# Bucketed attention and a rational feed-forward layer on one core: one weight load moved in the queue, and the last step's four banks finished and stored in turn

## The chip, the cores and the metric

The kernel runs on one core of one Trainium2 chip. The metric is the device time of one execution in microseconds. The core has five engines that this text names as the profile does: PE (TensorE, with its weight loads as PEld), DVE (VectorE), ACT (ScalarE), POOL (GpSimd) and SP (SyncE, which issues most of the DMAs; ACT issues a few).

## The reference, cut to what matters

Attention works on 4 batches of 8 heads, 768 rows, 64 columns. Every row of q and k falls into one of 64 buckets by the signs of six projections; a query sees only the keys of its own bucket. The result, seen as 3072 tokens of 512, goes through a feed-forward layer whose nonlinearity is a quotient of two polynomials.

```
mask   = q_bucket[:, :, :, None] == k_bucket[:, :, None, :]
scores = np.where(mask, scale * np.matmul(q, k.transpose(0, 1, 3, 2)), -1000000000.0)
attn   = np.exp(scores - np.max(scores, axis=-1, keepdims=True))
attn   = attn / (np.sum(attn, axis=-1, keepdims=True) + 1e-09)
x      = np.matmul(attn, v)            # as (3072, 512)
h      = x @ w_in                      # (3072, 2048)
P, Q   = a[0] + a[1]*h + a[2]*h2 + a[3]*h3,  1 + |b[0]| |h| + |b[1]| h2
out    = (P / (Q + 1e-6)) @ w_out      # (3072, 512)
```

The weights w_in and w_out are 64-bit floats; the kernel gets their bits as integers.

## The kernel before, in words

**Two stages.** The first (`attention`) takes the 32 heads as 16 pairs, 0 to 15, each in 12 steps of scores (two halves of the queries times six blocks of 128 keys). The second (`Ffn`) takes the tokens in 6 blocks of 512 (`NBLK`), each in 16 steps `f` of 128 hidden columns (`NFC`).

**How full precision is kept.** An operand is split into a high part in the format that PE takes and the rest, a low part; a product is the sum of high x high, high x low and low x high. So x becomes `xh` and `xl`, the quotient becomes `gh` and `gl`, and w_in and w_out become pairs too.

**A pair.** `maxstep` computes one block of scores of a later pair on PE into a PSUM tile `psm` and takes its row maxima on DVE (`m`). `shift_turn` turns the maxima with PE (`pst`), DVE writes them as `mt`, and `shift_rows` moves them by DMA into an extra row of the operand q (`q<-mt`: the rows of shifts). `scores` computes the blocks `pss` with two matmuls each, and ACT takes their exponential into one of seven buffers `E`. `values` multiplies `E` with `v` into `psv`, in groups of six steps (24 matmuls). POOL, and DVE in the last pairs, add up the `E` (`acc`) for the row sums (`psu`). From step 8 of pair 14 on, two of three score blocks (`wide`, `third`) use the PSUM tiles `psa`, two in number, which `psm` and `pst` use as well; the others use three tiles `s`.

**Operands of the next pair.** `second_low` and `second_high` copy parts of the split operands by DMA (`q<-lo`, `k<-lo`, `q<-q`, `k<-k`), `load_v` loads `v`, `values_store` writes the result of a pair to DRAM (`x_d<-xo`).

**Weights beside the attention.** `weights(i)` is a generator that brings one chunk of 128 x 512 of w_in (even `i`) or w_out (odd `i`): the load into `wr` (`wr<-w_in`, 512 KB), then from 64 to 32 bits with two ACT operations (`ws<-wr`, `wr<-wr`) and three on DVE (`wr<-wr`, `ws<-ws,wr`, and a custom instruction `ws<-wr,ws`), then the split: ACT casts the high part (`wi_hi<-ws`), DVE subtracts for the low one (`wi_lo`). There are two buffers `wr` and two `ws`. Two chunks go with every pair.

**First tokens.** While pairs 14 and 15 run, `Tokens.load` fetches the first block's x: `xl<-x_d` and `xh<-r_d` by DMA, the product `y` on DVE, the cast back to `xh` on ACT, and the subtraction into `xl` on DVE. `y` takes the buffer `lo0` or `lo1`, in which `second_low` finds its source.

**What sets the order.** Every engine carries out its instructions in the order in which the program emits them. In the attention stage this comes from the dictionary `plan` (lines 474 to 589): `at(p, s, f)` puts a piece of work at time 12 p + s, in units of steps, and the program is emitted in order of these times. The tables `MID`, `FIRST` and `LAST` hold the times. The chunk with index 28 = 2 * NFC - 4 is the w_in chunk of pair 14; its load stands at 1.44 steps into pair 14 (time 169.44). Each DMA takes one of eight semaphores in turn, and an issue waits until the DMA that had the semaphore before has landed.

**A step of the feed-forward stage.** `step(i)` emits the first product of step i (12 matmuls, `psh`), the polynomial terms on ACT and DVE, then for step i-1 the quotient (ACT: logarithm and exponential of the denominator, DVE: three operations, ending with `c<-w,c`), for step i-2 `parts` (ACT casts `gh`, POOL subtracts for `gl`, lines 705 to 710), and for step i-4 `gemm2`: 12 matmuls into four banks `pso`, one for each 128 tokens, two with gh and one with gl each, accumulated over the 16 steps. After the 16th step each bank is complete; `store` negates it into SBUF and stores it (`out<-o`).

**The end.** In the last two steps of the last block (`f >= NFC - 2`) all eight matmuls with gh come first and the four with gl last (line 718). ACT empties banks 0 and 2, DVE bank 1; bank 3 is split into two halves of 256 columns (`oh`): ACT empties the first and issues its store from its own queue, DVE the second, stored by SP.

Of the kernel before, what the change touches and what calls it, by code (L numbers as in the profile page):

```python
# [7 lines left out]
F32 = mybir.dt.float32  # L8
# [4 lines left out]
AF = mybir.ActivationFunctionType  # L13
ALU = mybir.AluOpType
# [4 lines left out]
P = 128  # L19
# [9 lines left out]
DM = 512  # L29
DFF = 2048  # L30
NCC = DM // P
NFC = DFF // P
NTK = 512
NBLK = TOK // NTK
# [27 lines left out]
LAST = dict(  # L62
    group=6, values=[0.28, 0.44], values_out=1.39, vout14=3.03,
    tokens=[[-15.0, -11.5, -8.6, -7.4], [-7.43, -5.11, -2.83, -1.09], [1.1, 4.2, 5.45, 6.3]], terms=1.0, ffn=[13.61, 16.09, 16.14],
    sums=16.96, wide=8, share=11, third=0, sums14=14.69, sumst14=22.46,
)
TINY = 2.0 ** -80

# [35 lines left out]
def bucket_attention_then_rational_ffn(ctx, tc, qT, kT, v, proj, w_in, w_out, coef, consts, out):  # L104
# [56 lines left out]
    def operands_to_terms():  # L161
# [3 lines left out]

    tail.tile([P, 32], F32, tag="below", name="below")
    last = attention(tc, nc, raw, ps_b, tail, tokens, early, operands_to_terms, ffn, load, QF, KF, v, w_in, w_out, wo_d, ident, cst,
                     ones, prj, wi_hi, wi_lo, x_d, s_d, r_d, coefficients)
    ffn.rest(ctx, last)
# [3 lines left out]
def attention(ctx, tc, nc, raw, ps_b, tail, tokens, early, operands_to_terms, ffn, load, QF, KF, v, w_in, w_out, wo_d, ident, cst, ones, prj,  # L173
# [305 lines left out]
    def spread(p, steps, gen):  # L479
        for s in steps:  # L480
            at(p, s, lambda g: next(g, None), gen)

    for p in range(NPAIR):
        mid = 0 < p < NPAIR - 1
        n = MID["group"] if mid else (FIRST if p == 0 else LAST)["group"]
# [36 lines left out]
    for i in range(2 * NFC):  # L522
        o = 12 * (i // 2)
        w = list(FIRST["weights"][i]) if i < 2 else list(MID["weights"][i % 2])
        if i == 2 * NFC - 1:
            w = w[:-4] + [w[-5] + x for x in MID["weights_last"]]
        spread(0, [o + x for x in w], weights(i))
# [134 lines left out]
class Ffn:  # L662
# [42 lines left out]
    def parts(self, t, f):  # L705
        p = self.state[t, f]
        gh, gl = self.tile("gh", t, f, 3, F32R), self.tile("gl", t, f, 3, F32R)
        self.nc.scalar.copy(gh, p)
        self.nc.gpsimd.tensor_tensor(out=gl, in0=p, in1=gh.bitcast(F32), op=ALU.subtract)
        self.state[t, f] = gh, gl  # L710

    def gemm2(self, t, f):
        nc = self.nc
        gh, gl = self.state.pop((t, f))
        n, end = NTK // P, (t, f) == (NBLK - 1, NFC - 1)

        order = [(i, k) for i in range(n) for k in range(3)]
        if t == NBLK - 1 and f >= NFC - 2:
            order.sort(key=lambda ik: ik[1] == 2)
        for i, k in order:  # L720
            if f == 0 and k == 0:
                self.sums[t, i] = self.ps_o.tile([P, DM], F32, tag="pso", name=f"pso{t}_{i}")
            g, w = ((gh, 0), (gh, 1), (gl, 0))[k]
            nc.tensor.matmul(self.sums[t, i], g[:, i * P : i * P + P], self.wo[f][:, w, :], start=(f == 0 and k == 0),
                             stop=(f == NFC - 1 and k == 2))
            if f == NFC - 1 and k == 2:
                if end and i == n - 1:
                    self.store(t, i, 0, DM // 2, "scalar", nc.scalar)
                    self.store(t, i, DM // 2, DM, "vector", nc.sync)
                else:  # L730
                    self.store(t, i, 0, DM, "vector" if end and i % 2 else "scalar", nc.sync)

    def store(self, t, i, c0, c1, engine, queue):
        nc = self.nc
        if c1 - c0 < DM:
            o = self.tp.tile([P, DM], F32, tag="h2", name=f"oh{c0}_{t}_{i}", bufs=2)[:, 0 : c1 - c0]
        else:
            tag, bufs = ("sr", 1) if i % 3 == 2 else ("xo", 2)
            o = self.rows.tile([P, DM], F32, tag=tag, name=f"o{t}_{i}", bufs=bufs)[:, 0 : c1 - c0]
        ps = self.sums[t, i][:, c0:c1]  # L740
        if engine == "scalar":
            nc.scalar.activation(o, ps, AF.Identity, scale=-1.0)
        else:
            nc.vector.tensor_scalar(out=o, in0=ps, scalar1=-1.0, scalar2=None, op0=ALU.mult)
        r0 = t * NTK + i * P
        queue.dma_start(self.out[r0 : r0 + P, c0:c1], o)

    def step(self, i):
        seq = [(t, f) for t in range(NBLK) for f in range(NFC)]
# [82 lines left out]
```

## Time and profile before

| what | value |
|---|---|
| time, median of 3 runs | 932.71 us (932.42 to 933.77) |
| the profiled execution's own time | 931.52 us |
| its span on the core | 929.7 us |
| PE busy | 920.8 us (99%) |
| DVE, ACT, POOL busy | 840.8 us (90%), 647.7 us (70%), 436.5 us (47%) |
| DMA queue of SP | 110.47 MB |
| granted clock of TensorE | 1.00 of full speed in all stretches up to 900 us |

Times in the profile count from the span's start. A row of the timeline gives start, duration, engine, the line (line 93 is that of a helper that issues all instructions, so instructions are told apart by their tiles), the operation, out<-in by the program's names, the shapes, how many instructions are merged in the row, and in brackets how long the engine stood idle before it and what ended that. A row of the busy times by stretches gives for one stretch its length, the busy time of PE, PEld, DVE, ACT and POOL with the number of instructions, the granted clock, the mean busy share of the 16 DMA engines, and GB/s. SPq and ACTq are the queues of these engines, and their rows show the issue of a DMA, not its transfer. In the text a time with a point such as 361.11 is a place in the span.

### The profile page before, as it was taken

Reading aid. Unit: us, or ns where it says so; the run is one execution under the profiler, and the core shown is the slowest. Engines: PE = TensorE matmul, PEld = TensorE weight load, DVE = VectorE, ACT = ScalarE, POOL = GpSimd, SP = SyncE. Lnnn points to the kernel's source line nnn. Section 1 sums busy time; section 2 is a strip of 40 time slices with the busy share of each in tenths; the row PEclk is TensorE's granted clock in tenths of the full one; section 3 lists DMA queues with packets and bytes.
Section 4 is the critical chain, followed back from the end, with each engine's and each line's share of the span. In section 5 each row is a group of like instructions: output and inputs, shape, how many; then the busy total and the mean of one; then the engine's idle time right before and its main releaser. Section 6 shows DMA issues by size and latency. Waiting matters only on the chain.

```text
span 929.7 us, 13698 instructions
## 1 busy us (share of the span) xinstructions
PE 920.8 (99%) x4678; PEld 699.3 (75%) x4678; DVE 840.8 (90%) x1029; ACT 647.7 (70%) x1229; POOL 436.5 (47%) x362
## 2 busy tenths in 40 slices
PE   8999999999999999999999999999999999999997
PEld 4666766666767676668888888888888888888886
DVE  6799889788988897887998999999999989998996
ACT  7567767676767676886777667776676677677664
POOL 5587878777878877622222232222223222222222
PEclk9999999999999999999999999999999999999999
DMA  6867877887877777545402100400040003001001
GB/s 197 213 182 225 229 221 230 214 232 220 232 218 220 220 193 228 166 158 189 165 1 86 51 1 1 136 1 0 1 137 1 1 38 98 1 1 46 1 1 46
DMA packets 51242, 111.57 MB, mean 120 GB/s; under 512 B 9346, under 2 KB 20214, under 8 KB 51172
## 3 DMA queue, kind: packets, MB, share of 16 engines
q1 hardware_dynamic: 50740, 110.47, 40.2%
q8 instruction: 37, 0.61, 0.3%
q14 instruction: 33, 0.27, 0.1%
q10 hardware_dynamic: 432, 0.23, 0.1%
HBM read 56.82 MB, written 21.17 MB: 84 GB/s over the span
## 4 chain that ended last, share of the span: by engine, by line
PE 92%; DVE 3%; DMA 3%; SPq 1%; issue 1%; ACT 1%; DVEq 0%; ACTq 0%
PE psh L93 28%; PE pso L93 28%; PE pss L93 13%; PE psv L93 12%; PE psm L93 7%; PE psu L93 2%; DVE m L93 2%; PE psb L93 1%; SPq L93 1%; DMA wr<-w_in 1%; DMA q<-q 1%; DVE ws L93 1%; DVE wr L93 0%; DMA qkf<-kT 0%; DMA xh<-r_d 0%
## 5 line engine op out<-in xcount | busy, mean ns | idle before, releaser
L93 POOL TENSOR_TENSOR gl<-c,gh 128x512 fp32r<-128x512 f32 x96 | 134.6, 1402 | 388.3 <-ACT gh L93 378.9
L93 ACT ACTIVATE E<-pss 128x384 f32<-128x384 f32 x384 | 167.7, 493 | 104.3 <-PE pss L93 93.8
L93 PE MATMUL pso<-wo,gh 128*128 128x512 f32 x768 | 235.5, 389 | 0.0
L93 DVE TENSOR_REDUCE m<-psm 128x1 f32<-128x768 f32 x192 | 179.4, 948 | 30.7 <-PE psm L93 27.6
L93 POOL TENSOR_TENSOR acc<-E,E 128x384 f32<-128x384 f32 x124 | 154.1, 1261 | 84.5 <-ACT E L93 84.4
L93 PE MATMUL pss<-q,k 128*128 128x384 f32 (+2 forms) x768 | 171.2, 346 | 0.4 <-ACT E L93 0.3
L93 PEld LDWEIGHTS pso<-wo,gh 128*128 128x128 f32 x768 | 144.1, 188 | 29.9
L93 PEld LDWEIGHTS pss<-q,k 128*128 128x128 f32 (+2 forms) x768 | 134.5, 189 | 29.2 <-issue 17.0
L93 PE MATMUL psh<-xh,wi_hi 128*128 128x512 f32 x384 | 149.6, 390 | 0.0
L93 PE MATMUL psh<-xl,wi_hi 128*128 128x512 f32 x384 | 149.4, 389 | 0.0
L93 PE MATMUL psh<-xh,wi_lo 128*128 128x512 f32 x384 | 149.4, 389 | 0.0
L93 PE MATMUL pso<-wo,gl 128*128 128x512 f32 x384 | 148.4, 389 | 0.0
L93 ACT ACTIVATE h<-psh 128x512 f32<-128x512 f32 x96 | 57.4, 598 | 127.5 <-PE psh L93 127.4
L93 POOL TENSOR_TENSOR acc<-acc,E 128x384 f32<-128x384 f32 x123 | 137.5, 1137 | 8.2 <-ACT E L93 8.0
L93 DVE SCALAR_TENSOR_TENSOR c<-c,ab,r 128x512 f32<-128x512 f32 x96 | 135.6, 1413 | 0.0
L93 PE MATMUL psv<-E,v 128*64 128x385 f32 x768 | 133.0, 492 | 0.0
L93 PE MATMUL psm<-k,q 76*128 76x384 f32 (+1 forms) x384 | 102.1, 349 | 1.9 <-DVE m L93 1.0
L93 PEld LDWEIGHTS psv<-E,v 128*64 128x64 f32 x768 | 52.4, 136 | 66.3 <-issue 63.2
L93 DVE SCALAR_TENSOR_TENSOR w<-h,absb,w 128x512 f32<-128x512 f32 x96 | 74.0, 771 | 16.1 <-ACT w L93 15.9
L93 PEld LDWEIGHTS psh<-xh,wi_hi 128*128 128x128 f32 x384 | 72.0, 187 | 16.2 <-issue 1.2
L93 PEld LDWEIGHTS psh<-xl,wi_hi 128*128 128x128 f32 x384 | 72.1, 188 | 15.0
L93 PEld LDWEIGHTS pso<-wo,gl 128*128 128x128 f32 x384 | 72.1, 188 | 15.0
(79 smaller groups left out, 1219.4 us busy)
## 6 DMA issues: line engine op xcount, KB each, us to landing
q<-q SPq DMA_DIRECT2D x45, 192.0 KB
k<-k SPq DMA_DIRECT2D x45, 192.0 KB
wr<-w_in SPq DMA_DIRECT2D x16, 512.0 KB
wr<-w_out SPq DMA_DIRECT2D x16, 512.0 KB
wo_d<-wr SPq DMA_DIRECT2D x16, 512.0 KB
wo<-wo_d SPq DMA_DIRECT2D x16, 512.0 KB
qkf<-qT SPq DMA_DIRECT2D x16, 384.0 KB
qkf<-kT SPq DMA_DIRECT2D x16, 384.0 KB
```

The lines of the kernel that those rows point to most:

```text
L93: return self.tc.keep_in_program_order(issue(*args, **kwargs))
```

## The change

Four things change.

1. The load of chunk 28 (`wr<-w_in`) gets its own time, -3.16 steps relative to pair 14, which is 8.84 steps into pair 13, just behind `shift_rows` of pair 14 (8.82). The other steps of the chunk keep their times.
2. In the last step of all (t = 5, f = 15), gl is subtracted on DVE and not on POOL.
3. In that step the matmuls come bank by bank (gh, gh, gl for each of the four banks); the step before keeps the order with gl last.
4. Bank 3 is emptied whole by ACT into one tile of 512 columns and stored by one DMA from ACT's queue; banks 0 to 2 are emptied by ACT, DVE and ACT and stored by SP, as before.

```
     sums=16.96, wide=8, share=11, third=0, sums14=14.69, weights14=-3.16, sumst14=22.46,
...
+        if i == 2 * NFC - 4:
+            w[0] = LAST["weights14"]
...
-        self.nc.gpsimd.tensor_tensor(out=gl, in0=p, in1=gh.bitcast(F32), op=ALU.subtract)
+        engine = self.nc.vector if (t, f) == (NBLK - 1, NFC - 1) else self.nc.gpsimd
+        engine.tensor_tensor(out=gl, in0=p, in1=gh.bitcast(F32), op=ALU.subtract)
...
-        if t == NBLK - 1 and f >= NFC - 2:
+        if t == NBLK - 1 and f == NFC - 2:
             order.sort(key=lambda ik: ik[1] == 2)
...
             if f == NFC - 1 and k == 2:
-                if end and i == n - 1:
-                    self.store(t, i, 0, DM // 2, "scalar", nc.scalar)
-                    self.store(t, i, DM // 2, DM, "vector", nc.sync)
-                else:
-                    self.store(t, i, 0, DM, "vector" if end and i % 2 else "scalar", nc.sync)
-
-    def store(self, t, i, c0, c1, engine, queue):
+                self.store(t, i, end, i == n - 1)
+
+    def store(self, t, i, end, last):
         nc = self.nc
-        if c1 - c0 < DM:
-            o = self.tp.tile([P, DM], F32, tag="h2", name=f"oh{c0}_{t}_{i}", bufs=2)[:, 0 : c1 - c0]
+        if end and last:
+            o = self.tp.tile([P, DM], F32, tag="h2", name=f"o{t}_{i}", bufs=2)
         else:
             tag, bufs = ("sr", 1) if i % 3 == 2 else ("xo", 2)
-            o = self.rows.tile([P, DM], F32, tag=tag, name=f"o{t}_{i}", bufs=bufs)[:, 0 : c1 - c0]
-        ps = self.sums[t, i][:, c0:c1]
-        if engine == "scalar":
-            nc.scalar.activation(o, ps, AF.Identity, scale=-1.0)
+            o = self.rows.tile([P, DM], F32, tag=tag, name=f"o{t}_{i}", bufs=bufs)
+        if end and i == 1:
+            nc.vector.tensor_scalar(out=o, in0=self.sums[t, i], scalar1=-1.0, scalar2=None, op0=ALU.mult)
         else:
-            nc.vector.tensor_scalar(out=o, in0=ps, scalar1=-1.0, scalar2=None, op0=ALU.mult)
+            nc.scalar.activation(o, self.sums[t, i], AF.Identity, scale=-1.0)
         r0 = t * NTK + i * P
-        queue.dma_start(self.out[r0 : r0 + P, c0:c1], o)
+        (nc.scalar if end and last else nc.sync).dma_start(self.out[r0 : r0 + P, :], o)
```

More of the change, by code (lines that the diff above doesn't have):

```diff
@@ L64 @@
     tokens=[[-15.0, -11.5, -8.6, -7.4], [-7.43, -5.11, -2.83, -1.09], [1.1, 4.2, 5.45, 6.3]], terms=1.0, ffn=[13.61, 16.09, 16.14],
-    sums=16.96, wide=8, share=11, third=0, sums14=14.69, sumst14=22.46,
+    sums=16.96, wide=8, share=11, third=0, sums14=14.69, weights14=-3.16, sumst14=22.46,
 )
```

## The prediction

> **What bounds the kernel now.** The page comes first, for the engine that is always busy.
>
> ```profile
> PE 920.8 (99%) x4678; PEld 699.3 (75%) x4678; DVE 840.8 (90%) x1029; ACT 647.7 (70%) x1229; POOL 436.5 (47%) x362
> ```
>
> TensorE (PE) sets the time, so an edit is worth what it takes out of PE's waits or out of the stretch after PE's last matmul. The busy time by stretches shows where those could lie.
>
> ```profile
> 300.00:400.00 100.00, 99.11 (x590) 67.03 (x590) 86.93 (x102) 72.34 (x165) 74.52 (x64) 1.00 0.67 197
> 800.00:900.00 100.00, 100.00 (x443) 82.81 (x442) 95.03 (x115) 68.85 (x116) 26.45 (x19) 1.00 0.03 11
> 900.00:930.00 30.00, 24.94 (x111) 20.30 (x109) 20.75 (x25) 14.69 (x25) 7.04 (x6) 0.99 0.10 36
> ```
>
> The feed-forward stage (from 400 us) has no idle PE until its end. There 30.00 - 24.94 = 5.06 us follow the last matmul, 4.8 of them inside the span of 929.7. In 300 to 400 PE shows 0.89 us idle, but a matmul's end is modelled, so the timeline of the weight loads (PEld) is the better witness. It shows one knot, while pair 14 runs:
>
> ```profile
> 357.98 1.18 SPq L93 DMA_DIRECT2D q<-lo  x2
> 361.11 0.54 SPq L93 DMA_DIRECT2D wr<-w_in  x1
> 361.92 1.01 DVE L93 TENSOR_TENSOR y<-xl,xh 128x768 f32<-128x768 f32 x1 [0.67 <-issue]
> 362.86 3.68 DVE L93 TENSOR_REDUCE m<-psm 128x1 f32<-128x768 f32 x4
> 363.86 0.30 PEld L93 LDWEIGHTS psm<-k,q 76*128 76x128 f32 x2
> 365.89 0.30 PEld L93 LDWEIGHTS pss<-q,k 77*128 77x128 f32 x2 [0.32 <-ACT E L93]
> 366.79 0.20 PEld L93 LDWEIGHTS psv<-E,v 128*64 128x64 f32 x4 [0.25 <-issue]
> 368.60 0.68 ACT L93 ACTIVATE ws<-wr 128x512 f32<-128x512 f32 x1 [2.38 <-DMA wr<-w_in]
> 369.32 0.43 DVE L93 TENSOR_SCALAR wr<-wr 128x512 int32<-128x512 int32 x1 [2.78 <-ACT ws L93]
> 369.43 0.14 PEld L93 LDWEIGHTS psv<-E,v 128*64 128x64 f32 x2 [0.18 <-issue]
> 369.77 0.84 ACT L93 ACTIVATE E<-pss 128x384 f32<-128x384 f32 x2
> 370.29 0.19 PEld L93 LDWEIGHTS psv<-E,v 128*64 128x64 f32 x2 [0.71 <-ACT E L93]
> 373.24 0.88 ACT L93 ACTIVATE E<-pss 128x384 f32<-128x384 f32 x2 [0.19 <-PE pss L93]
> 373.54 0.65 PEld L93 LDWEIGHTS pss<-q,k 77*128 77x128 f32 x4 [0.36 <-DVE m L93]
> 374.12 0.62 ACT L93 CAST wi_hi<-ws 128x512 fp32r<-128x512 f32 x1
> 374.65 0.87 ACT L93 ACTIVATE E<-pss 128x384 f32<-128x384 f32 x2
> 375.01 0.09 PEld L93 LDWEIGHTS pst<-cst,m 128*12 128x12 f32 x1 [0.81 <-DVE m L93]
> 375.01 2.04 PEld L93 LDWEIGHTS pss<-q,k 77*128 77x128 f32 x12
> ```
>
> The load `wr<-w_in` is issued at 361.11 and lands shortly before 368.60, some 7.5 us later. ScalarE (ACT) waits 2.38 us for it with an exponential E queued behind, and VectorE (DVE) 2.78 us with the maxima m queued behind. PE then waits for that E (0.71, where 0.18 is the usual gap of this loop) and twice for m (0.36 and 0.81): 0.53 + 0.36 + 0.81 = 1.70 us in one stretch.
>
> **The early load.** In SyncE's (SP) queue around the end of pair 13, this stands before (wr is the load, q_14<-mt the rows of shifts, q_15<-lo a part of the last pair's operands):
>
> ```order
> L93 DMA q_14_3674<-mt_None 1x12x128
> L93 DMA x_d_99<-xo_0_4151 128x384
> L93 DMA xl_4173<-x_d_86 128x512
> L93 DMA xh_4172<-r_d_106 64x512 x2
> L93 DMA xl_4173<-x_d_87 128x256
> L93 DMA xh_4172<-r_d_106 64x256 x2
> L93 DMA q_15_4181<-lo_15_3991 64x768 x2
> L93 DMA k_15_4182<-lo_15_4047 64x768 x2
> L93 DMA v_4209<-v 128x768
> L93 DMA wr_4265<-w_in 128x1024
> ```
>
> And with the change:
>
> ```order
> L93 DMA q_14_3674<-mt_None 1x12x128
> L93 DMA wr_4159<-w_in 128x1024
> L93 DMA x_d_99<-xo_0_4151 128x384
> L93 DMA xl_4176<-x_d_86 128x512
> L93 DMA xh_4175<-r_d_106 64x512 x2
> L93 DMA xl_4176<-x_d_87 128x256
> L93 DMA xh_4175<-r_d_106 64x256 x2
> L93 DMA q_15_4184<-lo_15_3991 64x768 x2
> ```
>
> One DMA has moved past twelve others; the seven compute instructions of that chunk stay where they were. The DMA engines' share (the figure before the last) shows what it moves out of and into:
>
> ```profile
> 352.00:354.00 2.00, 2.00 (x13) 1.96 (x12) 2.00 (x3) 1.81 (x6) 1.98 (x3) 1.00 0.09 33
> 366.00:368.00 2.00, 2.00 (x12) 1.17 (x14) 0.54 (x1) 0.22 (x1) 1.88 (x2) 1.00 1.03 233
> 352.97 0.45 SPq L93 DMA_DIRECT2D x_d<-xo  x1
> ```
>
> It is issued at 352.97 into 0.09 instead of at 361.11 into a full stretch, so I take it as landed by 361 even at the old 7.5 us. The waits of ACT and DVE go. E runs 2.4 us earlier, PE loses nothing at 370.29, and all behind it comes 0.53 sooner. What is late next is ACT: from 373.24 it has no gap, so its E at 374.65 comes only 0.53 sooner and ends at 375.52 - 0.53 = 374.99. Score block 10 needs the PSUM bank that this E reads. In the row at 375.01 its loads are the second four of twelve, at about 375.01 + 2.04 / 3 = 375.69, which was 0.17 after that E. So PE comes 0.53 + 0.17 = 0.70 us sooner there, not 1.70, though m no longer holds it.
>
> The price lies in the queue. All twelve DMAs are issued one issue later (0.54 by the load's row). The product y, at 361.92, overwrites a buffer that q<-lo reads, and DVE stood 0.67 idle before it, so I let y and the four maxima behind it come 0.55 late. The first of these ends about 363.8, just as PE loads at 363.86 for the block that needs its bank. PE so loses 0.55, of which the 0.32 that it waits for ACT at 365.89 anyway is taken back: 0.25 with rounding. V too is issued 0.55 later; PE takes it at 366.79 without a wait for it, and is itself 0.25 late by then, so between nothing and 0.30. I take nothing, that row being the nearest. The stage gives 0.70 - 0.25 = **0.45 us**, with ends of 0 (price 0.70) and 1.70 (no price, ACT not in the way). Pairs 14 and 15 keep their order behind it, and PE has no idle time from 400 to its end, so what is gained should stay.
>
> **The last step.** On PE, at the end of the program, the last step's matmuls (pso_0 to pso_3 are four banks) stood so:
>
> ```order
> L93 MATMUL pso_0_8657<-wo_4792,gh_15_9179 128x512 x2
> L93 MATMUL pso_1_8661<-wo_4792,gh_15_9179 128x512 x2
> L93 MATMUL pso_2_8665<-wo_4792,gh_15_9179 128x512 x2
> L93 MATMUL pso_3_8669<-wo_4792,gh_15_9179 128x512 x2
> L93 MATMUL pso_0_8657<-wo_4792,gl_15_9180 128x512
> L93 MATMUL pso_1_8661<-wo_4792,gl_15_9180 128x512
> L93 MATMUL pso_2_8665<-wo_4792,gl_15_9180 128x512
> L93 MATMUL pso_3_8669<-wo_4792,gl_15_9180 128x512
> ```
>
> and now stand so:
>
> ```order
> L93 MATMUL pso_0_8657<-wo_4792,gh_15_9179 128x512 x2
> L93 MATMUL pso_0_8657<-wo_4792,gl_15_9180 128x512
> L93 MATMUL pso_1_8661<-wo_4792,gh_15_9179 128x512 x2
> L93 MATMUL pso_1_8661<-wo_4792,gl_15_9180 128x512
> L93 MATMUL pso_2_8665<-wo_4792,gh_15_9179 128x512 x2
> L93 MATMUL pso_2_8665<-wo_4792,gl_15_9180 128x512
> L93 MATMUL pso_3_8669<-wo_4792,gh_15_9179 128x512 x2
> L93 MATMUL pso_3_8669<-wo_4792,gl_15_9180 128x512
> ```
>
> gl_15, made by DVE now and no longer by GpSimd (POOL), is needed by the third matmul, not the ninth, and each bank is finished before the next. Bank 3 is emptied whole, where before DVE's half of it stood 0.48 us for ACT's half. The timeline of the end before:
>
> ```profile
> 918.60 1.57 POOL L93 TENSOR_TENSOR gl<-c,gh 128x512 fp32r<-128x512 f32 x1 [2.12 <-ACT gh L93]
> 919.06 1.67 DVE L93 SCALAR_TENSOR_TENSOR c<-w,c 128x512 f32<-128x512 f32 x1
> 920.81 0.62 ACT L93 CAST gh<-c 128x512 fp32r<-128x512 f32 x1 [2.34 <-DVE c L93]
> 921.83 1.77 PEld L93 LDWEIGHTS pso<-wo,gh 128*128 128x128 f32 x8
> 922.05 1.98 PE L93 MATMUL pso<-wo,gh 128*128 128x512 f32 x8
> 923.87 1.07 PE L93 MATMUL pso<-wo,gl 128*128 128x512 f32 x4
> 924.29 1.09 ACT L93 ACTIVATE o<-pso 128x512 f32<-128x512 f32 x2 [2.86 <-PE pso L93]
> 924.92 1.31 SPq L93 DMA_DIRECT2D out<-o  x3
> 925.69 0.42 DVE L93 TENSOR_SCALAR oh<-pso 128x256 f32<-128x256 f32 x1 [0.48 <-ACT oh L93]
> 926.32 0.41 SPq L93 DMA_DIRECT2D out<-oh  x1
> 925.00:926.00 1.00, 0.00 (x0) 0.00 (x0) 0.52 (x2) 0.66 (x2) 0.00 (x0) 1.00 0.23 90
> 928.00:929.00 1.00, 0.00 (x0) 0.00 (x0) 0.00 (x0) 0.00 (x0) 0.00 (x0) 1.00 0.45 156
> ```
>
> gh ends at 921.43. A subtraction of this size on DVE is this row:
>
> ```profile
> 369.66 0.68 DVE L93 TENSOR_TENSOR wr<-ws,wr 128x512 fp32r<-128x512 f32 x1
> ```
>
> so gl ends near 922.15. PE's third weight load is due at 921.83 + 2 x 0.22 = 922.27: no wait, with 0.12 to spare. If DVE took the 1.67 of 919.06, while POOL ran, PE would stand for 0.85 and pass it on whole; POOL has nothing left to run then, and I take 0. [...]
>
> Matmuls start 0.227 apart, so the banks end at 922.9, 923.6, 924.3 and 924.94, and PE's end is unmoved. ACT (0.60 each) and DVE empty them as they come; only the last is left at 924.94, and its store is issued at about 924.98 + 0.60 + 0.03 = 925.61, against 926.32. How long it then takes no row shows alone. Before, data began at about 926 - 0.23 = 925.77, 0.85 after the first issue, and ended at 928.45, so four stores' worth took 2.68, 0.67 for 256 KB, back to back. Now each store is ready 0.68 after the one before, so none should queue: the last one's data ends at 925.61 + 0.85 + 0.67 = 927.13, 1.3 sooner. If it started as late after its issue as the last did before, only 0.71 - 0.33 (twice the bytes) = 0.38 is gained. I take **1.2 us**, near the first, since no data is left to stand in front; a late gl could make it 0.35.
>
> [...]
>
> **Rivals.** The profiled execution took 931.52 us, 1.19 under the median of 932.71; differences are applied to both alike. The sum, 0.45 + 1.2 = 1.65, gives 929.87 by the profile and 931.06 by the median. About 0.2% (1.87 us) is what a measurement here can tell from no change.
> - Full recovery: ACT is not in the way and the queue costs little. 1.2 to 1.70 + 1.2 gives 2.4 to 2.9, or 930.3 to 929.8. For it: the 2.4 us of idle ACT. Against: ACT without a gap from 373.24.
> - The load only moves the wait: the queue's delay takes the whole 0.70. 1.2 remain: 931.5. For it: DVE's 0.67 before y, and the edge at 363.86.
> - The last store keeps its latency: 0.45 + 0.38 = 0.83, 931.9.
> - Slower: the queue stands behind the load. SP did wait for it once:
>
> ```profile
> SPq L93 <- DMA wr<-w_in: 1.1, 1, 1.1
> ```
>
> That was eight DMAs behind the load. The eighth behind it is now the first q<-lo. If the load again takes 7.5 us, that is issued at 360.5, not 357.98, 2.5 late; add 512 KB at the 233 GB/s above, 2.2, and y is 4.7 late. PE loses 4.7 - 0.30, gains 0.70 and 1.2: 2.5 us slower, 935.2. Slower at all from a delay of 2.2. Against it: the share of 0.09.
>
> **How the numbers follow.** Forecast 48% (its own range 930.6 to 931.6), full recovery 13%, load without effect 18%, store's latency 14%, slower 7%. Above 1.87 us of gain lie the full recovery and some two fifths of the forecast: faster 0.34. Slower 0.07. The rest, 0.59, is within 0.2%. The range goes from the full recovery's 929.9 to 932.6, which takes in the smaller gains and the runs' own scatter (932.42 to 933.77); the slower case and a part of the scatter are left out.
>
> **What would show it.** Right: ACT's ws and DVE's wr near 366 to 367 without a DMA wait, no wait for E in that psv block, pss waiting for ACT E once near 375, y some 0.5 late; at the end gl on DVE before 922.3 (shifted by the gain), four evictions one after another, and the closing stretch after PE's last matmul near 3.8 us instead of 4.8. Wrong: y over 2 us late, a wait of psv for V, or a closing stretch that is as long as before.

## The result and the profile after

The changed kernel takes 934.76 us (median of 20 runs, 931.52 to 937.38) beside 932.10 for the kernel before (20 runs, 930.61 to 934.02): a ratio of 1.0027, 95% interval 1.0018 to 1.0035. It is slower by 2.6 us, where 1.65 us of gain was forecast.

One thing is needed to read the numbers. Each run also has the mean clock granted to TensorE over its span. For the changed kernel 17 of 20 runs stand at 0.998 or below, down to 0.996, and those take 932.96 to 937.38 us. Its profiled execution happens to be the one run at 1.000. It takes 931.52 us, span 929.7, the time of the profiled execution of the kernel before. So I read first what that profile shows, and then what the other runs add.

Two marks split a span into parts that can be compared: the start of the psu block in which pair 13's row sums are made (PE, near 362 us), and the first matmul of the feed-forward stage (psh<-xh,wi_hi, near 400). What lies ahead of the first mark differs by up to 3.6 us between the profiles below, by 2.9 between two of one kernel (e_y_later and its repeat), and hides a change of 1 us. So it is partly chance that the two profiled executions take the same time. The kernel before, timeline, start and duration in us:

```profile
361.71 1.50 PE L93 MATMUL psu<-acc,ones 128*32 128x384 f32 x16
400.69 0.49 PE L93 MATMUL psh<-xh,wi_hi 128*128 128x512 f32 x1
```

The changed kernel, the same view, with what the prediction's steps speak of:

```profile
353.22 0.45 SPq L93 DMA_DIRECT2D wr<-w_in  x1
357.67 2.00 SPq L93 DMA_DIRECT2D q<-lo  x2
362.09 1.50 PE L93 MATMUL psu<-acc,ones 128*32 128x384 f32 x16
363.97 1.29 DVE L93 TENSOR_TENSOR y<-xl,xh 128x768 f32<-128x768 f32 x1 [2.33 <-DMA k<-lo]
365.18 3.68 DVE L93 TENSOR_REDUCE m<-psm 128x1 f32<-128x768 f32 x4
366.18 0.62 PE L93 MATMUL psm<-k,q 76*128 76x384 f32 x2 [1.69 <-DVE m L93]
368.01 0.66 ACT L93 ACTIVATE ws<-wr 128x512 f32<-128x512 f32 x1
368.78 0.42 DVE L93 TENSOR_SCALAR wr<-wr 128x512 int32<-128x512 int32 x1
401.88 0.50 PE L93 MATMUL psh<-xh,wi_hi 128*128 128x512 f32 x1
922.63 0.69 DVE L93 TENSOR_TENSOR gl<-c,gh 128x512 fp32r<-128x512 f32 x1 [0.74 <-ACT gh L93]
923.45 0.19 PEld L93 LDWEIGHTS pso<-wo,gl 128*128 128x128 f32 x1
925.46 1.28 ACT L93 ACTIVATE o<-pso 128x512 f32<-128x512 f32 x2 [0.76 <-PE pso L93]
926.77 0.35 ACTq L93 DMA_DIRECT2D out<-o  x1
```

From mark to mark it is 401.88 - 362.09 = 39.79 us, where it was 400.69 - 361.71 = 38.98. From psh to the end of the span it is 929.7 - 401.88 = 527.82, where it was 529.01. The last step gives 1.19 us, and in this pair of profiles the attention stage takes 0.81 of it back; the other 0.38 lies ahead of the first mark, within what differs there anyway. The 0.81 is rough: in four profiles with this part of the kernel unchanged (before, c_before, e_end and e_end_gl_pool below) the stretch is 38.64 to 39.52 us, so against them the change's profiled execution loses 0.3 to 1.2 there. The waits of ACT and DVE for the load are gone (no bracket at 368.01 and 368.78), but a new one is there: DVE stands 2.33 us in front of y, the four maxima m stand behind y, and PE waits 1.69 us for the first of these.

In the windows of both kernels the column before the last is the DMA engines' share. Before:

```profile
356.00:358.00 2.00, 2.00 (x16) 0.82 (x12) 1.60 (x2) 0.00 (x0) 2.00 (x2) 1.00 0.46 143
358.00:360.00 2.00, 2.00 (x13) 1.68 (x10) 0.31 (x1) 0.87 (x2) 0.35 (x1) 1.00 0.62 163
```

After:

```profile
356.00:358.00 2.00, 2.00 (x16) 0.88 (x14) 1.66 (x2) 0.18 (x1) 2.00 (x2) 1.00 1.02 379
358.00:360.00 2.00, 2.00 (x13) 1.40 (x10) 0.00 (x0) 0.56 (x2) 0.42 (x1) 1.00 0.95 258
```

The early load did not use up an idle share: it moved its 512 KB in front of the token rows and of q<-lo, and these now come through full engines (shares of 1.02 and 0.95, where 0.46 and 0.62 stood before). SyncE's queue waited too, for a load of token rows (its waits over 345 to 372; no such row stands there before):

```profile
SPq L93 <- DMA xl<-x_d: 0.8, 1, 0.8
```

### The profile page after: what moved, and what is told of

It is laid out like the page before. It is cut to its first block, busy times and chain, and to the rows that moved or that the text cites. A ratio compares the mean times of both kernels' runs of the same rounds, so it can differ in the third digit from the quotient of the medians.

```text
span 929.7 us, 13694 instructions
## 1 busy us (share of the span) xinstructions
PE 920.8 (99%) x4678; PEld 699.6 (75%) x4678; DVE 844.5 (91%) x1029; ACT 647.5 (70%) x1229; POOL 436.5 (47%) x361
## 4 chain that ended last, share of the span: by engine, by line
PE 92%; DVE 5%; issue 1%; SPq 1%; ACT 1%; DMA 0%; DVEq 0%; ACTq 0%
PE psh L93 28%; PE pso L93 28%; PE pss L93 13%; PE psv L93 12%; PE psm L93 7%; DVE m L93 3%; PE psu L93 2%; PE psb L93 1%; DVE ws L93 1%; SPq L93 1%; PE psw L93 0%; DVE wr L93 0%; DVE lo L93 0%; ACT E L93 0%; DMA wo_d<-wr 0%
## 5 line engine op out<-in xcount | busy, mean ns | idle before, releaser
L93 PEld LDWEIGHTS psh<-xh,wi_lo 128*128 128x128 f32 x384 | 72.2, 188 | 14.9
```

Of the source, the lines that this page charges most:

```text
L93: return self.tc.keep_in_program_order(issue(*args, **kwargs))
```

## The experiments

Theory at the outset (Q, later S): the early load makes y late, DVE stands at y, PE waits for the maxima behind it. Whether the lower clock is no part of the change or its consequence (C) was open. Rivals: the new end brings it (E), or other late transfers do (D). All runs are in one table; "low" counts runs at a granted clock of 0.998 or below (two runs of over 1000 us are left out of the counts), and the last two columns are the profiled execution's two parts.

| run | median us | kernel before, run beside it | ratio, 95% | low | psu to psh | psh to end |
|---|---|---|---|---|---|---|
| c_before | 931.92 | 931.72 | 0.9991 to 1.0008 | 1 of 11 | 39.25 | 529.04 |
| c_after | 934.30 | 931.72 | 1.0018 to 1.0044 | 11 of 12 | 43.83 | 527.91 |
| e_load | 935.47 | 931.72 | 1.0027 to 1.0051 | 5 of 5 | 43.83 | 529.11 |
| e_end | 930.81 | 931.72 | 0.9982 to 1.0002 | 0 of 11 | 39.52 | 527.81 |
| e_y_later | 930.44 | 932.88 | 0.9970 to 0.9988 | 1 of 12 | 38.36 | 527.82 |
| e_keep_busy | 932.60 | 932.88 | 0.9992 to 1.0016 | 2 of 12 | 40.56 | 528.02 |
| e_load_behind_k | 935.15 | 932.88 | 1.0000 to 1.0032 | 9 of 12 | 38.83 | 527.84 |
| e_rows_later | 931.46 | 932.88 | 0.9977 to 0.9995 | 1 of 12 | 38.74 | 527.89 |
| e_y_later_old_load | 932.01 | 932.39 | 0.9985 to 1.0010 | 1 of 11 | 38.47 | 527.89 |
| e_y_later_again | 930.73 | 932.39 | 0.9968 to 0.9993 | 0 of 12 | 38.31 | 527.83 |
| e_load_behind_k_again | 934.78 | 932.39 | 1.0012 to 1.0044 | 8 of 12 | 40.22 | 527.81 |
| e_end_gl_pool | 932.17 | 932.39 | 0.9982 to 1.0010 | 1 of 11 | 38.64 | 528.34 |
| e_behind_k_busy | 935.64 | 931.84 | 1.0022 to 1.0048 | 4 of 12 | 40.24 | 531.63 |
| e_y_later_v_first | 928.91 | 931.84 | 0.9961 to 0.9990 | 0 of 7 | 37.84 | 527.87 |
| e_behind_k_look1 | 933.75 | 931.80 | one run | 0.998 | 41.96 | 527.88 |
| e_behind_k_look2 | 931.07 | 931.80 | one run | 1.000 | 39.55 | 527.87 |

**The two halves, and controls.** The kernel before, unchanged:

> The kernel before, unchanged, as a control that lists span and granted clock of each of its runs. Theory Q (the load that stands earlier makes y late, and nothing else costs): its clock is 1.000 in some runs and 0.996 to 0.999 in others just as the changed kernel's is, so the clock is no part of the change; ratio 1.000. Theory C (the changed kernel's slower runs are clock runs that the change itself brings on): here all runs show 1.000.

The changed kernel, again:

> The changed kernel again, in the same call as its two halves: ratio 1.002 to 1.0035. Theory Q: its runs at the full clock are within 0.5 us of the kernel before (the profile: 1.2 lost behind y, 1.2 won at the end), and slower ones show a clock below 1. Theory C: no run at a clock of 0.996 is under 934.

Only the load moved (the diff's two hunks on weights14), with the old end:

> Only the load stands earlier; the end is the old one. Theory Q: q<-lo issues late by 1 to 2 us as in the changed kernel, PE waits 1.5 to 2.0 us near 366, the attention stage is 1.2 us longer, the closing stretch 4.8; +1.2 us at the full clock, so 933.3 against 932.1, and more (+3.8) if the later load also brings the slower runs. Rival E (the end brings the slower runs): +1.2 at every clock. My forecast before the result would give -0.45.

Only the end, with the load where it was:

> Only the end is the new one; the load stands where it stood. Theory Q: no wait of PE near 366, attention stage as before, closing stretch 3.6: -1.2 us, 930.9 against 932.1. Rival E (the end brings the slower runs, by bank order, gl on DVE or the whole last store): -1.2 in a run at full clock, but a median 1 to 3 us above the kernel before.

The load alone costs 3.75 us, the end alone takes 0.9 off, which its interval does not tell from nothing; but its profile shows it (527.81 from psh to the end, where the kernel before has 529.04). The unchanged kernel has one low run in 11, the load alone five in five, the end alone none: the lower clock comes with the early load, and rival E falls. Theory C's sign held as well: no run of c_after at 0.996 or below is under 934 us (lowest 934.23). The profile of c_after is one of those runs, and shows where. Its timeline:

```profile
358.72 1.40 SPq L93 DMA_DIRECT2D q<-lo  x2
361.96 1.50 PE L93 MATMUL psu<-acc,ones 128*32 128x384 f32 x16
364.35 1.62 DVE L93 TENSOR_TENSOR y<-xl,xh 128x768 f32<-128x768 f32 x1 [2.83 <-DMA k<-lo]
366.89 0.61 PE L93 MATMUL psm<-k,q 76*128 76x384 f32 x2 [2.53 <-DVE m L93]
371.00 5.85 PE L93 MATMUL psv<-E,v 128*64 128x385 f32 x24
405.79 0.50 PE L93 MATMUL psh<-xh,wi_hi 128*128 128x512 f32 x1
```

And its windows; the column behind the engines' busy times is the granted clock:

```profile
366.00:367.00 1.00, 0.11 (x1) 0.11 (x1) 1.00 (x2) 0.83 (x1) 0.00 (x0) 1.00 1.08 227
367.00:368.00 1.00, 1.00 (x6) 1.00 (x7) 1.00 (x2) 0.04 (x1) 0.00 (x0) 0.87 1.00 229
368.00:369.00 1.00, 1.00 (x5) 1.00 (x5) 0.57 (x1) 0.85 (x3) 0.47 (x1) 0.50 0.99 314
...
374.00:375.00 1.00, 1.00 (x6) 0.38 (x4) 1.00 (x2) 0.00 (x0) 0.00 (x0) 0.71 0.00 0
360.00:380.00 20.00, 17.47 (x89) 11.77 (x87) 14.21 (x16) 10.46 (x24) 10.09 (x9) 0.83 0.72 203
```

PE has waited 2.53 us here instead of 1.69, and after it resumes, its clock falls to half and stays there until 374.6. The mean over 360 to 380 is 0.83, so 0.17 x 20 = 3.4 us of full-rate work are lost, which is 6.8 us at half rate. A psv block of 24 matmuls takes 5.85 us, where it takes 4.10 at full clock. The load alone shows the same picture, with a mean clock of 0.83 over 360 to 380 as well:

```profile
363.47 1.29 DVE L93 TENSOR_TENSOR y<-xl,xh 128x768 f32<-128x768 f32 x1 [3.16 <-DMA k<-lo]
365.68 0.62 PE L93 MATMUL psm<-k,q 76*128 76x384 f32 x2 [2.52 <-DVE m L93]
```

**Wait or clock.** Eighteen small matmuls, whose results nobody reads, fill PE's wait:

```diff
+    def keep_busy(n):
+        ps = ps_b.tile([P, 512], F32, tag="v", name="psk")
+        idb = ident.bitcast(BF16)
+        for _ in range(n):
+            nc.tensor.matmul(ps[:, 0:256], idb[:, 0:P], idb, start=True, stop=True)
...
+    at(NPAIR - 3, 15.16, keep_busy, 18)
```

> The changed kernel, with 18 added small matmuls on PE (about 2 us of work on a bank that is free there, results not used) in the place where it waits for the maxima. The wait of the program stays. Theory S (the clock's half rate is the larger part of the loss, and it comes from PE being idle): clock 0.999 to 1.000 in all runs, 931.5 to 932.8. Rival W (the loss is the wait itself, and the lower clock only goes along with it): still 934 to 935.

It came out nearly as theory S has it: 932.60 us, with ten of 12 runs, not all, at 0.999 or 1.000. The timeline:

```profile
362.12 1.50 PE L93 MATMUL psu<-acc,ones 128*32 128x384 f32 x16
364.36 2.14 PE L93 MATMUL psk<-cst 128*128 128x256 bf16 x18
364.51 1.60 DVE L93 TENSOR_TENSOR y<-xl,xh 128x768 f32<-128x768 f32 x1 [2.83 <-DMA q<-lo]
367.04 0.62 PE L93 MATMUL psm<-k,q 76*128 76x384 f32 x2 [0.53 <-DVE m L93]
402.68 0.50 PE L93 MATMUL psh<-xh,wi_hi 128*128 128x512 f32 x1
```

y starts 2.39 us after psu, to the hundredth as late as in c_after (364.35 - 361.96), and the program's own wait is not shortened: the psm block comes 4.92 us after psu, in c_after 4.93. Yet the stretch takes 40.56 us instead of 43.83, and the clock over 360 to 380 is 1.00 instead of 0.83. The difference of 3.3 us is the price of the half rate, near the 3.4 read from the clock above. The wait itself costs 40.56 - 39.25 = 1.3, or 1.0 to 1.9 against the four profiles with the old load.

**What stands in the way.** All transfers stay as late, but DVE does three maxima before y:

```diff
-    tokens=[[-15.0, -11.5, -8.6, -7.4],
+    tokens=[[-15.0, -8.7, -8.0, -7.0],
```

> The changed kernel, with only y of the first token block (and the two steps behind it) put behind three maxima of pair 15 on DVE; all DMAs keep their order and are as late as before. Theory S (DVE stands at y until q<-lo has read y's buffer, three maxima stand behind it, PE waits 2 to 2.9 us for them, and then the clock halves for some 6 us): no PE wait above 0.7 us near 366, clock 0.999 to 1.000, no run above 933; 930.2 to 931.3. Rival D (the earlier load delays PE by what else lands late: k<-lo, V, q<-q): PE waits 1.5 us or more in the same stretch for another releaser, and the median stays at 933 or above.

And again, beside its counterpart:

> The changed kernel with y later, again, in one call with its counterpart with the old load: ratio 0.997 to 0.9988, clock 0.999 to 1.000 in nearly all runs.

Both came out as expected, with ratios of 0.9979 and 0.9980, but for one run of the first at 933.61 (clock 0.998), where none above 933 was expected. DVE does not stand at y any more:

```profile
363.40 1.81 DVE L93 TENSOR_REDUCE m<-psm 128x1 f32<-128x768 f32 x2
366.72 0.96 DVE L93 TENSOR_REDUCE m<-psm 128x1 f32<-128x768 f32 x1 [1.50 <-PE psm L93]
367.59 0.95 DVE L93 TENSOR_TENSOR y<-xl,xh 128x768 f32<-128x768 f32 x1
369.27 4.10 PE L93 MATMUL psv<-E,v 128*64 128x385 f32 x24 [0.48 <-DMA v<-v]
```

PE now waits 0.48 us for V. The counterpart has the late y and the new end, but the load at its old place (weights14 out):

> The new end, y of the first token block behind the three maxima, but the load where it stood before the change. Tells what the early load is worth once y doesn't stand in its way. By the prediction's own term (0.45 net of a 0.25 price for y, so 0.70 with y out of the way): 0.7 us slower than the kernel with y later and the early load, about 931.1 where that gives 930.4. Rival N (the load's place is worth nothing, ACT has no gap to use it in): the same time. Rival Y (y itself was the cost, also before the change): the same time and both 1 us or more below the end alone.

Its median, 932.01, is 1.3 us above the 930.73 of the kernel with the early load, where 0.7 was expected. By the profiles the early load is worth only 38.47 - 38.31 = 0.16 us between the marks (0.11 by the first profile), and nothing behind them; the rest, if it is real, lies ahead of the first mark, where one kernel's profiles differ by more. What the early load is worth while PE still waits for V therefore stays open. Putting the token rows behind V as well:

```diff
-    tokens=[[-15.0, -11.5, -8.6, -7.4],
+    tokens=[[-12.9, -8.7, -8.0, -7.0],
```

> As the kernel with y later, and the token rows too are loaded behind V, so that q<-lo comes right behind the load. Theory S: q<-lo and k<-lo land 2 us sooner than in the kernel before, the load is as early as in the changed kernel, V sooner as well: 929.8 to 931. Rival D: no better than the kernel with y later alone, or slower if y, now waiting for its rows, stands in front of the ninth maximum.

931.46 lies above the expected 929.8 to 931. No PE wait for V is left, but y now waits 1.61 us for its rows (released by xh<-r_d), and the stretch is 0.4 us longer than with y later alone. That speaks for the second half of the rival, though the two ratios' intervals overlap.

**The load at another place, and a second wait.** Between k<-lo and V:

```diff
-    sums=16.96, wide=8, share=11, third=0, sums14=14.69, weights14=-3.16, sumst14=22.46,
+    sums=16.96, wide=8, share=11, third=0, sums14=14.69, weights14=-1.5, sumst14=22.46,
```

> The changed kernel, with the load issued behind q<-lo and k<-lo and ahead of V (0.6 us sooner than before the change). Theory S: q<-lo lands as before, y is on time, no 2 us wait of PE; V lands 0.5 to 1.5 later than before and the first psv block may wait for it by as much; 930.3 to 932. Rival D: any load ahead of V brings the long wait: 934.

y was on time, but 935.15 us is far from theory S's 930.3 to 932. The profiled run had a clock of 1.000 and shows no long wait. The same kernel again:

> The load between k<-lo and V, again, since its profile showed a good run (929.5, V 1.0 us late at the first psv block) and 9 of its 12 runs a clock of 0.996 to 0.998. Theory S, widened (any long wait of PE in this stretch halves the clock; here it is the wait for V): a profile of a slow run shows psv waiting for V by 1.5 us or more and the clock at 0.5 behind it; 934 to 936. Rival: the wait stands elsewhere in the program, or the clock falls without a wait.

Again the profiled run was at full clock, although V is 2.07 us late for PE:

```profile
369.09 4.10 PE L93 MATMUL psv<-E,v 128*64 128x385 f32 x24 [2.07 <-DMA v<-v]
```

(The 1.0 and 2.4 us in the next text are these two profiles' waits by the weight load's rows, 0.98 and 2.39; by the matmuls' rows they are 0.66 and 2.07.) Then with PE kept busy in front of psv:

```diff
-    at(NPAIR - 3, 15.16, keep_busy, 18)
+    at(NPAIR - 3, 17.5, keep_busy, 18)
```

> The kernel with the load between k<-lo and V, with 18 added small matmuls (2.1 us, results not used) in front of the first psv block, where its profiles show PE waiting for V by 1.0 and by 2.4 us. Theory S, widened: its slow runs (8 and 9 of 12 at a clock of 0.995 to 0.998) come from PE standing idle for V there; with PE kept busy nearly all runs show 0.999 to 1.000, and the median falls from 934.8 to 935.2 to between 931 and 933. Rival: the clock falls for another reason or at another place, then at least half of the runs stay at 0.998 or below and the median at 934 or above.

This one missed: low runs fell to 4 of 12, a part of what theory S expects, but the median stayed at 935.64, as the rival has it. Three of the eight runs at 0.999 or 1.000 took 935.5 to 936.2 us, so something besides the clock costs time here. Its profile shows a loss 400 us away from the load: a store of the result landed late, ACT stood for it, PE for ACT, and the clock fell there (0.91 over 760 to 780).

```profile
770.21 0.60 ACT L93 ACTIVATE o<-pso 128x512 f32<-128x512 f32 x1 [3.58 <-DMA out<-o]
770.86 0.74 PE L93 MATMUL pso<-wo,gh 128*128 128x512 f32 x2 [1.89 <-ACT o L93]
```

In every other profile the longest wait of ACT for a store in that stage is 1.2 or 1.6 us. Two single runs of the kernel without the filling, each with its profile, were to tell the one from the other:

> One look at the kernel with the load between k<-lo and V, of which 17 of 24 timed runs showed a clock of 0.995 to 0.998 and both profiles 1.000. Theory S, widened: a profile at 0.998 or below shows PE waiting 2.5 us or more for V at the first psv block, and the clock at 0.5 for some 6 us behind it. Rival F: the wait and the lower clock stand in the FFN stage, where one store of the result lands late (as in the profile of the kernel with PE kept busy), and have nothing to do with the load.

> The same look once more, for the case that the other profile falls on a run at full clock: the same expectations.

The first ran at 0.998, and theory S holds: V comes 2.49 us late for PE, psv takes 5.44 us where it takes 4.10 at full clock, and the mean clock over 360 to 380 is 0.91.

```profile
369.81 5.44 PE L93 MATMUL psv<-E,v 128*64 128x385 f32 x24 [2.49 <-DMA v<-v]
```

```profile
360.00:380.00 20.00, 17.07 (x95) 11.40 (x94) 14.50 (x17) 12.01 (x29) 12.32 (x10) 0.91 0.74 218
```

The second, at full clock, has a wait of 1.38 and a psv block of 4.10:

```profile
368.41 4.10 PE L93 MATMUL psv<-E,v 128*64 128x385 f32 x24 [1.38 <-DMA v<-v]
```

So the same load that made y late from one place makes V late from the other. Why the median did not fall with the filling is left open; the late store explains the profiled run alone.

**The end.** gl of the last step made by GpSimd again, the rest of the new end kept, without the early load:

```diff
-        engine = self.nc.vector if (t, f) == (NBLK - 1, NFC - 1) else self.nc.gpsimd
-        engine.tensor_tensor(out=gl, in0=p, in1=gh.bitcast(F32), op=ALU.subtract)
+        self.nc.gpsimd.tensor_tensor(out=gl, in0=p, in1=gh.bitcast(F32), op=ALU.subtract)
```

> The new end alone, but gl of the last step made by GpSimd again, behind its gl of the step before. By the prediction's step: gl is ready at about 923.0 by the kernel before's times, PE needs it at 922.27, so PE waits 0.7 us and the end comes 0.7 to 0.85 later than with the end alone: 931.5 against 930.8. Rival: the wait is hidden behind the evictions and stores, and the end is as early as with gl on DVE.

```profile
922.71 1.28 POOL L93 TENSOR_TENSOR gl<-c,gh 128x512 fp32r<-128x512 f32 x1 [1.39 <-issue]
924.05 0.19 PEld L93 LDWEIGHTS pso<-wo,gl 128*128 128x128 f32 x1 [0.65 <-POOL gl L93]
```

PE's weight load waits 0.65, and psh to end is 528.34 - 527.81 = 0.53 longer than with the new end alone: the expected wait, a little smaller. The move of gl to DVE is worth that much of the 1.19.

**A version that beats both.** y later, and V of pair 14 loaded ahead of q<-lo and k<-lo:

```diff
-            at(p - 1, (MID if p > 1 else FIRST)["load_v"], load_v, p)
+            at(p - 1, 9.7 if p == NPAIR - 2 else (MID if p > 1 else FIRST)["load_v"], load_v, p)
```

> The kernel with y later, and V of pair 14 loaded ahead of q<-lo and k<-lo (both have time: their readers come later). Its wait of PE for V (0.5 to 0.8 us) goes: 0.3 to 0.8 us faster than with y later alone, about 930. Rival: k<-lo and q<-lo, 0.7 us later, make ACT or the first score block late, and nothing is gained.

```profile
366.04 0.52 PE L93 MATMUL psm<-k,q 76*128 76x384 f32 x2
366.49 4.10 PE L93 MATMUL psv<-E,v 128*64 128x385 f32 x24
370.51 0.97 PE L93 MATMUL pss<-q,k 77*128 77x384 f32 x4
```

PE goes from psm to psv without a wait, and the stretch is 37.84, 0.5 less than with y later alone. It takes 928.91 us beside 931.84, with no run of seven at a lower clock. By the medians it is 2.9 us faster than the kernel before, by the ratio of 0.9975 (0.9961 to 0.9990) 2.3.

## Why the prediction was wrong

**The early load's gain (0.70): the waits went, the gain did not come.** ACT and DVE no longer wait for the load, as forecast. The step "What is late next is ACT" did not come to pass: m and then V came next. With both out of the way (e_y_later_v_first) the stretch is 38.47 - 37.84 = 0.63 us shorter than with y later and the old load. That is near the 0.70, but it is the worth of two moves together: V ahead with the old load was not tried.

**The price (0.25): this step failed.** The prediction said "The price lies in the queue" and let y come 0.55 late, one issue. But y starts 1.88 us after psu (c_after 2.39, e_load 2.71) where it started 0.21 after it, so it is 1.7 to 2.5 us late. Little of that is the issue: the row that issues the two q<-lo ends 362.09 - 359.67 = 2.42 us ahead of psu, where it was 361.71 - 359.16 = 2.55. In c_after and e_load it ends 0.7 us later than that, in e_keep_busy 0.5 sooner, and there y is as late as in c_after. What was late was the data. At the 379 and 233 GB/s that full engines moved (the rows at 356 and, in the prediction, at 366) the load's 512 KB take an estimated 1.4 to 2.2 us. I had counted what the load was issued into (a share of 0.09), not whose bytes stood behind it. The profile names k<-lo as the last of y's releasers, and in e_keep_busy q<-lo; by the program y takes the buffer lo0, which q<-lo reads and k<-lo does not. Whether y's token rows were there sooner was not separated.

**What no step had: the clock.** By the prediction's own rule for a late y (delay less 0.30 of slack, less 0.70 and 1.2 of gains) a delay of 1.7 to 2.5 would have come out between 0.5 us faster and 0.3 slower, and the profiled execution at full clock, with 0.0, lies there. The other runs add the half rate that came behind PE's wait (2.53 us in c_after), 3.3 us where it was isolated (c_after beside e_keep_busy). That turns no change into 2.6 us slower. No term of the prediction stood for it.

**V (taken as no wait):** right for the change's own place, where PE takes V without a wait in the profile; wrong as a rule, since y later alone uncovers 0.48 us, and the load behind k<-lo 0.66 to 2.5.

**The last step (1.2): right, term by term.** gl ends at 922.63 + 0.69 = 923.32 and PE loads it at 923.45: 0.13 to spare, 0.12 forecast. The last store is issued at 926.77; the forecast 925.61, shifted by psh's 1.19, is 926.80. The data end at about 928.34, forecast 927.13 + 1.19 = 928.32:

```profile
928.00:929.00 1.00, 0.00 (x0) 0.00 (x0) 0.00 (x0) 0.00 (x0) 0.00 (x0) 0.93 0.34 129
```

From psh to the end it is 1.19 us shorter (1.2 forecast), and the table agrees: 529.01 to 529.11 with the old end; 527.81 to 528.02 with the new one, apart from e_end_gl_pool and the late store of e_behind_k_busy. Whether the last store stood behind the third one's data was not separated.

**The rivals.** The slower one, "the queue stands behind the load", was given 7% and had the right place. Of its two terms the data's 2.2 us was about right; the issue's 2.5 was 0.7 at most, so it sized y's delay at 4.7, about twice too much. Its time, 935.2, is near the measured 934.76 by luck: the half rate, of which it knew nothing, makes up for the difference. Of the signs named as wrong, "y over 2 us late" showed in c_after and e_load (2.2 and 2.5); in the first profile y was 1.7 late.

## What to carry to other kernels

Before a load is moved ahead, list what is queued behind it by bytes, not by issues, and who stands behind each of these in the order of its engine. Here DVE stood 2.33 to 3.16 us at y (after, c_after, e_load), with four maxima behind it that did not need y. Where that reached TensorE, a wait of 2.53 us (c_after) cost 3.3 us beyond itself, so put the instruction that can wait behind those that can't before moving the load. And compare stretches between two marks of the program, but learn the scatter of each first: from psh to the end 13 profiles with the new end hold to 527.81 to 528.02 us, from psu to psh four profiles of the unchanged part differ by 0.9, and the medians of the kernel before by 1.2 (931.72 to 932.88).

## What the runs showed of the hardware

PE waits of 1.38, 1.69 and 2.07 us (e_behind_k_look2, the change's first profile and e_load_behind_k_again) left the clock at 1.00; waits of 2.49, 2.52 and 2.53 (e_behind_k_look1, e_load and c_after) went with half rate, and so did the 1.89 of the late store (e_behind_k_busy). So the length of the wait alone does not decide: 1.89 was enough once, 2.07 was not. In three of these four profiles the fall came after PE had resumed: near 367.7 in c_after, 366.7 in e_load and 771.7 in e_behind_k_busy (0.87 over the stretch of 1 us in each), where PE resumed at 366.89, 365.68 and 770.86. In e_behind_k_look1 it came sooner: 0.91 over 365 to 370 is an estimated 0.9 us at half rate, so from near 369.1, and PE resumed at 369.81. Added up over stretches of 1 us, the half rate lasted 6.8 us in c_after and in e_load (a mean of 0.83 over 20 us in both) and 3.4 us in e_behind_k_busy; over stretches of 5 us it comes to 3.5 in e_behind_k_look1 (a mean of 0.91 over 20 us in both). Why it lasted twice as long in the first two was not tested.

A transfer's lateness varied from run to run: PE's wait for V in four profiles of one kernel (e_load_behind_k, its repeat, e_behind_k_look1 and e_behind_k_look2) was 0.66, 2.07, 2.49 and 1.38 us, with the same order in the queue.
